# Two TensorE details of a four-layer kernel: logit sums by row halves, and an evenly shared tail in the output projection

## Chip, cores and metric

The kernel runs on one core of one Trainium2 chip. The metric is the device time of one execution in microseconds (us), lower is better; a program is timed several times and the median is compared. Times of single instructions and waits come from one profiled execution.

## What is computed

Four residual layers on a sequence of S = 2048 rows of width D = 576: attention, gated unit, attention, gated unit, with the same weights in both rounds.

```python
x = x + A(layernorm(x)); x = x + B(layernorm(x)); x = x + A(layernorm(x)); x = x + B(layernorm(x))

def A(x):                       # 32 heads of 18, window of 8 positions, every second one
    q, k, v = split(x @ wqkv)
    logits[h, s, w] = sum_d q[h, s, d] * k[h, s - 2 * w, d] * 18 ** -0.5      # masked before the start
    attn = softmax(logits, over w)
    return (sum_w attn[h, s, w] * v[h, s - 2 * w, :]) @ wo

def B(x):                       # F = 4608
    return ((x @ w_gate) * (x @ w_up)) @ w_down
```

## The kernel before

**Chunks.** The sequence is cut into chunks: the first four (j = 0 to 3) have 128 rows, the other fourteen (j = 4 to 17) have 256. A chunk j is one attention layer (`attention`) and the gated unit behind it (`glu`). Chunks of the first and of the second round alternate in groups of 1024 rows.

**Layout.** D = 576 is four full blocks of 128 and a tail of 64. The weights of the projections are permuted so that partition 32 * jj + h of a block holds head h; a block holds four of the 18 elements of each head, and the tail holds two, in its lower 64 partitions. The upper 64 partitions of the tail block (index KF = 4) are zero in q, k, v and, until the change, in `wo_p`.

**TensorE by row halves.** In chunks of 256 rows most products are issued as pairs: the helper `both` (L438) zips two lists, one of products that use partitions 0 to 63 (row half 0) and one for partitions 64 to 127 (row half 1). The two halves write different PSUM banks. Each bank gets contributions from both halves, so the work is done in two passes with the banks swapped, and between the passes a `fence` (L443) stands: ScalarE copies one element of the bank (L445, tile `tok`), and the first product of the second pass waits for that copy.

**PSUM slots.** Four slots `unit`, each of a bank in `pg` and its partner in `pu` (the fourth is `acct` and `pa`), are shared by all that runs on TensorE from j = 5 on: gated units (two slots a pair of units), projections (two), output projection (two), and the logit sums (one).

**The logits.** VectorE multiplies q by shifted k (L641) and adds blocks (L645 to L650), which leaves four tiles `s1` of 128 partitions. TensorE then sums over the partitions that belong to one head with a 0/1 matrix `Esel` (L656): 16 products of 128 rows by 32 columns, four of them side by side in the four column groups. The sums stand in one PSUM bank. `soft1` (L672) takes the maximum over the window (L676) and subtracts it into `Lt` (L677); ScalarE's exponential (L679), `soft2` (L683, L684) and `soft3` (L687) follow. In chunks of j >= 5 the result goes through DRAM to be spread (L707 to L712), and 15 VectorE operations (L727, L741) apply it to v and leave `oT`.

**The output projection of a chunk of 256 rows** (L752 to L774). `strip(i, r, hh, first)` lists the products of row half r for rows i and output half hh: five for r = 0 (four blocks and the tail), four for r = 1, since the tail stands in the lower partitions alone. Pass 1 gives row half 0 the first output half and row half 1 the second; pass 2 swaps them. VectorE adds the result to the residual (L751).

**Order of the work.** Nothing runs in the order of the program text: `op` records operations with an engine, a cost in ns, what they read and write, a priority and a slot to hold, and `Plan.run` (L79) writes each engine's queue by simulating those costs. The products of the gated units are a fixed chain (`bb`); attention is fitted in between, some chunks ahead. The plan adds TURN (L25) when TensorE goes between operations marked `half` and others. Each engine's queue then runs in that order on the chip, whatever the real durations.

Of the kernel before, what the change touches and what calls it, by code (L numbers as in the profile page):

```python
# [156 lines left out]
def kernel(  # L157
# [148 lines left out]
    def setup_b():  # L306
        def mk_zero():
            for t_ in qT_:
                nc.gpsimd.memset(t_[TL:P, KF, :], 0.0)
            for t_ in kv_:  # L310
                nc.gpsimd.memset(t_[TL:P, :, KF, :], 0.0)
            nc.gpsimd.memset(q_x[TL:P, KF, :], 0.0)
            nc.gpsimd.memset(kv_x[TL:P, :, KF, :], 0.0)
            for t_ in halo:
                nc.gpsimd.memset(t_[:], 0.0)
            nc.gpsimd.memset(wo_p[TL:P, KF, :], 0.0)
        op("POOL", 2600, mk_zero, w=[f"{x}{t}{i}" for x in "qkv" for t in (4, "H") for i in ZN] + [f"halo{i}" for i in range(n_al)] + ["wo_z"])
        for k in range(KT):
# [41 lines left out]
    def setup_wo():  # L360
# [3 lines left out]
        for dd in range(2):  # L364
            op("SP", 470, dma(wo_p[32 * dd:32 * dd + 32, KF, :], wv_[:, 16 + dd, :]), w=[f"wot{dd}"], nbytes=32 * D * 2, prio=2)

# [9 lines left out]

    wok = ["wo_z", "wot0", "wot1"] + [f"wo{dd}" for dd in range(4)]

# [88 lines left out]
    def attention(j, la, t0, nst):  # L467
# [164 lines left out]
        if not on_pe:  # L632
            pool["k"] = "unit"
        b1 = Bank()
        for p_ in range(W // 2):
            def l1(p_=p_):
# [15 lines left out]
            def esel(p_=p_, srcs=None):  # L652
                pav = wv(b1())
                for i_, s_ in enumerate(srcs()):
                    for jj in range(4):
# [12 lines left out]
        if not fast:  # L668
            op("PE", 250 + 4 * max(45, 0.215 * n), lambda: [esel(p_, lambda p_=p_: [late["s1"][p_]]) for p_ in range(W // 2)],
               r=["sel", "s10", "s11", "s12", "s13"], prio=0, margin=mg, **b1.take())  # L670
# [7 lines left out]
        op("DVE", 260 + 4.2 * n + (250 if t0 == 0 else 0), soft1, r=[b1.key] + (["cap"] if t0 == 0 else []), w=["Lt", "mx"], prio=prio - 1, **b1.drop())  # L678
        op("ACT", 109 + 1.66 * n, lambda: nc.scalar.activation(late["Lt"][:, 0:W * sq], late["Lt"][:, 0:W * sq], ACT.Exp),  # L679
# [72 lines left out]
        if nst == 2:  # L752
# [4 lines left out]
            def strip(i, r, hh, first):  # L757
                def one(t):
                    rows = slice(TL * r, TL * r + TL)
                    return nc.tensor.matmul(bank(hh, us[i])[:, 0:HD], lhsT=oT[rows, t, i * P:(i + 1) * P], rhs=wo_p[rows, t, hh * HD:(hh + 1) * HD],  # L760
                                     start=(first and t == 0), stop=(not first and t >= KF - 1), skip_group_check=True)
# [296 lines left out]
```

## Time and profile before

| what | value |
| --- | --- |
| time, median of 3 runs | 1064.89 us (1063.15 to 1067.89) |
| the profiled execution's own time | 1063.73 us |
| its span, first to last instruction | 1061.6 us, granted TensorE clock 0.996 |
| TensorE busy (PE) | 1036.8 us, 98% of the span |
| VectorE busy (DVE) | 782.6 us, 74% |
| ScalarE busy (ACT) | 407.5 us, 38% |
| GpSimd busy (POOL) | 16.4 us, all of it in the first 19 us |

How to read it: a busy TensorE is not TensorE at its peak, because the shown duration of a product reaches from its start to the end of its results and overlaps with the next ones. What counts on TensorE is the distance from one start to the next. Queues run in order, so a wait at the head of a queue holds all that stands behind it.

### The profile page before, as it was taken

The numbers are of one execution on the slowest core, as the hardware profiler recorded it, in microseconds if no ns is written. First come the engines' busy times: TensorE is split into PE (matmuls) and PEld (weight loads), VectorE is DVE, ScalarE is ACT, GpSimd is POOL, SyncE is SP. The second block draws the span as 40 slices with busy tenths as digits, with TensorE's granted clock in tenths as the row PEclk, the third lists the DMA queues.
The fourth block names the chain that finished last, engine by engine and source line by source line (L and its number), as shares of the span: only waits on it lengthen the run. The fifth ranks groups of instructions, "written<-read, shape, count | busy, mean of one in ns | idle before, by whom it ended". The sixth has DMA issues, their size and how long they took to land.

```text
span 1061.6 us, 39889 instructions
## 1 busy us (share of the span) xinstructions
PE 1036.8 (98%) x17832; PEld 834.5 (79%) x17832; DVE 782.6 (74%) x1420; ACT 407.5 (38%) x1080; POOL 16.4 (2%) x43
## 2 busy tenths in 40 slices
PE   5999999999999999999999999999999999999998
PEld 4787887788788889778888787877887788777775
DVE  6788998877989969797979753676788847733332
ACT  4742254244444453334433333334344252233231
POOL 6000000000000000000000000000000000000000
PEclk8999999999999999999999999999999999999999
DMA  9955554463335633335552534243252344343332
GB/s 267 333 170 166 183 148 134 130 143 111 82 107 103 163 76 123 107 94 121 141 130 69 154 99 105 90 128 94 84 158 82 98 90 125 115 127 102 117 99 68
DMA packets 146827, 133.67 MB, mean 126 GB/s; under 512 B 42272, under 2 KB 146016, under 8 KB 146656
## 3 DMA queue, kind: packets, MB, share of 16 engines
q1 hardware_dynamic: 146656, 131.13, 44.0%
q8 instruction: 139, 2.28, 0.9%
q14 instruction: 32, 0.26, 0.1%
HBM read 118.51 MB, written 4.06 MB: 115 GB/s over the span
## 4 chain that ended last, share of the span: by engine, by line
PE 75%; DVE 18%; DMA 4%; issue 1%; ACT 1%; SPq 1%; DVEq 0%; ACTq 0%
PE pu L855 14%; PE pg L855 14%; PE acct L855 5%; PE pu L923 5%; PE pa L923 5%; PE pa L855 5%; PE pg L923 4%; PE acct L923 4%; DVE scr L727 3%; DVE oT L741 3%; PE pg L501 3%; DVE h L867 3%; PE pu L501 3%; PE pu L831 3%; PE pg L831 2%; DVE scr L641 2%
## 5 line engine op out<-in xcount | busy, mean ns | idle before, releaser
L855 PEld LDWEIGHTS <-wg 64*128 64x128 bf16 x4032 | 366.4, 94 | 29.5 <-issue 2.9
L855 PE MATMUL pg<-xnT_B,wg 64*128 64x256 bf16 x3008 | 386.5, 269 | 0.9 <-DVE xf L751 0.9
L855 PE MATMUL pu<-xnT_B,wu 64*128 64x256 bf16 x3008 | 385.9, 269 | 0.3
L855 PEld LDWEIGHTS <-wu 64*128 64x128 bf16 x4032 | 365.7, 94 | 22.6 <-issue 1.0
L923 PEld LDWEIGHTS <-h 64*128 64x128 bf16 (+1 forms) x1992 | 118.1, 94 | 99.4 <-DVE h L867 2.7
L867 DVE TENSOR_TENSOR h<-pu,g_sb 128x512 bf16<-128x512 f32 x224 | 150.9, 685 | 55.3 <-ACT g_sb L866 51.9
L924 PE MATMUL pu<-wd,h 64*128 64x64 bf16 (+1 forms) x972 | 183.7, 189 | 1.0 <-DVE h L867 0.9
L924 PE MATMUL pg<-wd,h 64*128 64x64 bf16 (+1 forms) x972 | 183.8, 189 | 0.0
L866 ACT CAST g_sb<-pg 128x512 bf16<-128x512 f32 x224 | 130.0, 586 | 131.7 <-PE pg L855 87.6
L445 ACT COPY tok<-pu 1x1 f32<-1x1 f32 x276 | 40.6, 147 | 300.2 <-PE pu L855 202.8
L855 PE MATMUL acct<-xnT_B,wg 64*128 64x256 bf16 x1024 | 139.8, 269 | 0.0
L855 PE MATMUL pa<-xnT_B,wu 64*128 64x256 bf16 x1024 | 139.3, 269 | 0.1
L923 PE MATMUL pg<-wd,h 64*128 64x512 bf16 x528 | 136.4, 377 | 0.3 <-DVE h L867 0.3
L923 PE MATMUL pu<-wd,h 64*128 64x512 bf16 x528 | 136.5, 377 | 0.0
L923 PE MATMUL acct<-wd,h 64*128 64x512 bf16 (+1 forms) x468 | 121.3, 377 | 1.4 <-DVE h L867 1.4
L923 PE MATMUL pa<-wd,h 64*128 64x512 bf16 (+1 forms) x468 | 121.5, 377 | 0.0
L501 PEld LDWEIGHTS <-wqkv 64*128 64x128 bf16 (+1 forms) x2044 | 106.6, 96 | 15.7 <-issue 4.8
L924 PEld LDWEIGHTS <-h 64*128 64x128 bf16 (+1 forms) x1992 | 116.5, 95 | 0.8 <-issue 0.2
L641 DVE TENSOR_TENSOR scr<-qT,kv 128x2560 bf16<-128x2560 bf16 (+1 forms) x68 | 91.1, 1343 | 25.9 <-ACT kv L576 25.9
L501 PE MATMUL pg<-xnT_A,wqkv 64*128 64x256 bf16 (+2 forms) x916 | 103.6, 265 | 2.0 <-ACT xnT_A L430 2.0
L501 PE MATMUL pu<-xnT_A,wqkv 64*128 64x256 bf16 (+1 forms) x876 | 101.8, 267 | 0.3 <-DVE kv L574 0.3
L855 PE MATMUL pg<-xnT_B,wgu_t 64*128 64x256 bf16 x376 | 101.1, 269 | 0.0
(149 smaller groups left out, 1580.1 us busy)
## 6 DMA issues: line engine op xcount, KB each, us to landing
wd<-in_B_w_down_dram SPq DMA_DIRECT2D x324, 288.0 KB, 4.6
scr<-a_dram SPq DMA_DIRECT2D x52, 128.0 KB, 2.7
wg<-in_B_w_gate_dram SPq DMA_DIRECT2D x6, 768.0 KB, 10.2
wu<-in_B_w_up_dram SPq DMA_DIRECT2D x6, 768.0 KB, 11.0
out_dram<-xf SPq DMA_DIRECT2D x16, 144.0 KB, 3.8
xb<-in_A_x_dram SPq DMA_DIRECT2D x6, 288.0 KB, 2.8
a_dram<-scr SPq DMA_DIRECT2D x13, 128.0 KB, 2.4
scr<-in_A_wqkv_dram SPq DMA_DIRECT2D x4, 288.0 KB, 4.8
```

The lines of the kernel that those rows point to most:

```text
L445: box["at"] = nc.scalar.copy(tok[0:1, :], src())
L501: return nc.tensor.matmul(bank(p_, u)[0:m, e * n:(e + 1) * n], lhsT=wqkv[r_, k, w0:w0 + m], rhs=xnT_A[r_, k, c0:c0 + n], start=start, stop ...
L641: nc.vector.tensor_tensor(late["prod"][p_ % 2][:, :, :, 0:n], q2, k2, op=ALU.mult)
L727: nc.vector.tensor_tensor(js(dst), js(vT[:, :, o0:o0 + n]), abw, op=ALU.mult)
L741: op("DVE", 70 + 2.63 * n, lambda i_=i_: nc.vector.tensor_tensor(oT[:, :, 0:n], oT[:, :, 0:n], late["prod"][i_ % 2][:, 0, :, 0:n], op=ALU. ...
L831: nc.tensor.matmul(pt[:, e * n:(e + 1) * n], lhsT=w_[:, k, ft * P:(ft + 1) * P], rhs=xT[:, k, 0:n], start=(first and k == 0 and e == 0), s ...
L855: return nc.tensor.matmul(ps[:, e * n:(e + 1) * n], lhsT=w_, rhs=xT[rows, k, 0:n], start=(first and e == 0 and k == 0), stop=(not first an ...
L866: op("ACT", 490, lambda: nc.scalar.copy(g_sb[gs][:, 0:ul], pg[use["slot"]][:, 0:ul]), r=[f"wg_{j}_{u}"], w=[f"g{gs}"], prio=0, due=True)
L867: op("DVE", 605, lambda: nc.vector.tensor_tensor(hb[hs][:, 0:ul], pu[use["slot"]][:, 0:ul], g_sb[gs][:, 0:ul], op=ALU.mult), r=[f"wu_{j}_{ ...
L923: return [lambda: nc.tensor.matmul((pg, pu)[i][use["slot"]][:], lhsT=lhs, rhs=wt[rows, e % 2, 0:512], start=first, stop=fin, skip_group_ch ...
L924: lambda: nc.tensor.matmul((pg, pu)[i][tl["slot"]][:, 0:TL], lhsT=lhs, rhs=wt[rows, e % 2, 512:D], start=first, stop=fin, skip_group_check ...
```

## The change

1. **Logit sums of chunks j >= 5** (`split`): each of the 16 products is cut into two of 64 rows by 32 columns, one for each row half, so there are 32. Row half 0 writes the bank in `pg`, row half 1 its partner in `pu` of the same slot. ScalarE copies the `pg` bank into `Lt`; `soft1` adds the `pu` bank to it on VectorE, and its maximum and its subtraction now read `Lt` in SBUF. The plan marks the TensorE operation as `half`.
2. **Output projection of the 14 chunks of 256 rows**: the tail rows of `wo` are loaded a second time into the upper 64 partitions (two DMAs more), in place of a memset to zero. ScalarE copies the tail of `oT` for the second 128 rows into the upper partitions. The tail of the first 128 rows is then done by row half 0, that of the second 128 by row half 1: the strips have 5 and 4 products for i = 0, and 4 and 5 for i = 1. The strip with five goes first in each zip, and the fence reads the bank that it wrote.

```diff
-            nc.gpsimd.memset(wo_p[TL:P, KF, :], 0.0)
...
         for dd in range(2):
-            op("SP", 470, dma(wo_p[32 * dd:32 * dd + 32, KF, :], wv_[:, 16 + dd, :]), w=[f"wot{dd}"], nbytes=32 * D * 2, prio=2)
+            for r_ in (0, TL):
+                op("SP", 470, dma(wo_p[r_ + 32 * dd:r_ + 32 * dd + 32, KF, :], wv_[:, 16 + dd, :]), w=[f"wot{dd}{r_}"], nbytes=32 * D * 2, prio=2)
...
+        split = not on_pe
...
+                if split:
+                    s_ = srcs()[0]
+                    for jj in range(4):
+                        for r_, t_ in ((slice(0, TL), pav), (slice(TL, P), wv(pu[b1.use["slot"]]))):
+                            nc.tensor.matmul(t_[32 * jj:32 * jj + 32, 2 * p_:2 * p_ + 2, :], lhsT=Esel[r_, :], rhs=s_[r_, :, sq * jj:sq * (jj + 1)],
+                                             start=(p_ == 0), stop=True, skip_group_check=True)
+                    return
...
+        if split:
+            op("ACT", 490, lambda: nc.scalar.copy(wv(late["Lt"]), wv(b1())), r=[b1.key], w=["Lt"], prio=prio - 1)
...
             pav = wv(b1())
+            if split:
+                lt = wv(late["Lt"])
+                nc.vector.tensor_tensor(lt, lt, wv(pu[b1.use["slot"]]), op=ALU.add)
+                pav = lt
...
-                return [lambda t=t: one(t) for t in range(KF + 1 - r)]
+                return [lambda t=t: one(t) for t in range(KF + (i == r))]
+            op("ACT", 280, lambda: nc.scalar.copy(oT[TL:P, KF, P:2 * P], oT[0:TL, KF, P:2 * P]), r=["oT"], w=["oTt"], prio=prio)
...
-                    o = op("PE", KT * TILE * HD, lambda i=i, first=first: both(strip(i, 0, 0 if first else 1, first), strip(i, 1, 1 if first else 0, first),
-                                                                                           None if first else fs[i]),
+                    o = op("PE", (KF + 0.5) * TILE * HD, lambda i=i, first=first: both(*[strip(i, r, r if first else 1 - r, first) for r in (i, 1 - i)],
+                                                                                      None if first else fs[i]),
...
-                        fence(fs[i], lambda i=i: bank(0, us[i])[0:1, 0:1], [f"wo{j}_{i}"])
+                        fence(fs[i], lambda i=i: bank(i, us[i])[0:1, 0:1], [f"wo{j}_{i}"])
```

More of the change, by code (lines that the diff above doesn't have):

```diff
@@ L315, in mk_zero @@
                 nc.gpsimd.memset(t_[:], 0.0)
-            nc.gpsimd.memset(wo_p[TL:P, KF, :], 0.0)
-        op("POOL", 2600, mk_zero, w=[f"{x}{t}{i}" for x in "qkv" for t in (4, "H") for i in ZN] + [f"halo{i}" for i in range(n_al)] + ["wo_z"])
+        op("POOL", 2600, mk_zero, w=[f"{x}{t}{i}" for x in "qkv" for t in (4, "H") for i in ZN] + [f"halo{i}" for i in range(n_al)])
         for k in range(KT):
@@ L375, in setup_glu @@
             op("SP", 550, dma(wgu_t[TL:2 * TL, fs], B_w_up[KF * P:D, fs]), w=[f"wut{s}"], nbytes=TL * fw * 2, prio=4 + s)
-    wok = ["wo_z", "wot0", "wot1"] + [f"wo{dd}" for dd in range(4)]
+    wok = [f"wot{dd}{r_}" for dd in range(2) for r_ in (0, TL)] + [f"wo{dd}" for dd in range(4)]
     def head(src, keys, nst, dst, key, prio, ab, on_pe, mg, c0=0, halves=False):
@@ L669, in attention @@
             op("PE", 250 + 4 * max(45, 0.215 * n), lambda: [esel(p_, lambda p_=p_: [late["s1"][p_]]) for p_ in range(W // 2)],
-               r=["sel", "s10", "s11", "s12", "s13"], prio=0, margin=mg, **b1.take())
+               r=["sel", "s10", "s11", "s12", "s13"], prio=0, margin=mg, half=split, **b1.take())
+        if split:
+            op("ACT", 490, lambda: nc.scalar.copy(wv(late["Lt"]), wv(b1())), r=[b1.key], w=["Lt"], prio=prio - 1)
         def soft1():
             pav = wv(b1())
+            if split:
+                lt = wv(late["Lt"])
+                nc.vector.tensor_tensor(lt, lt, wv(pu[b1.use["slot"]]), op=ALU.add)
+                pav = lt
             if t0 == 0:
@@ L677, in soft1 @@
             nc.vector.tensor_tensor(wv(late["Lt"]), pav, mx_t[:, 0:sq].unsqueeze(1).to_broadcast([P, W, sq]), op=ALU.subtract)
-        op("DVE", 260 + 4.2 * n + (250 if t0 == 0 else 0), soft1, r=[b1.key] + (["cap"] if t0 == 0 else []), w=["Lt", "mx"], prio=prio - 1, **b1.drop())
+        op("DVE", 260 + 4.2 * n + (250 if t0 == 0 else 0) + (600 if split else 0), soft1, r=[b1.key] + (["Lt"] if split else []) + (["cap"] if t0 == 0 else []), w=["Lt", "mx"], prio=prio - 1, **b1.drop())
         op("ACT", 109 + 1.66 * n, lambda: nc.scalar.activation(late["Lt"][:, 0:W * sq], late["Lt"][:, 0:W * sq], ACT.Exp),
```

## The prediction

> **What bounds the kernel now.** I read the page's busy rows, the table of windows, the waits of TensorE, and then the timeline around the two places that change.
>
> ```profile
> span 1061.6 us, 39889 instructions
> PE 1036.8 (98%) x17832; PEld 834.5 (79%) x17832; DVE 782.6 (74%) x1420; ACT 407.5 (38%) x1080; POOL 16.4 (2%) x43
> ...
> PE 75%; DVE 18%; DMA 4%; issue 1%; ACT 1%; SPq 1%; DVEq 0%; ACTq 0%
> ```
>
> TensorE is never long without work, and three quarters of the chain that ended last are its own. The windows say where VectorE comes close (columns: window, its length, busy us of PE, PEld, DVE, ACT, POOL):
>
> ```profile
> 120.00:640.00 520.00, 515.36 (x8938) 421.01 (x8937) 438.98 (x770) 213.56 (x575) 0.00 (x0) 1.00 0.44 118
> 640.00:1000.00 360.00, 358.55 (x6334) 284.59 (x6332) 227.61 (x397) 126.24 (x353) 0.00 (x0) 1.00 0.38 108
> ```
>
> VectorE is 84% busy (439 of 520) up to 640 us and 63% after it; attention is prepared ahead there. TensorE waits for VectorE seldom (waits of TensorE, total us, times, longest):
>
> ```profile
> PE acct L923 <- DVE h L867: 1.4, 2, 0.8
> PE pu L924 <- DVE h L867: 0.9, 2, 0.7
> ...
> PE pg L855 <- DVE xf L751: 0.9, 2, 0.6
> ```
>
> So time is won where TensorE's stream gets shorter, and lost where its queue stands for a PSUM slot or an `h`.
>
> **Part 1, the output projection.** The timeline of the one at 728.77 us, its last rows (start, length):
>
> ```profile
> 730.86 0.28 PE L760 MATMUL pa<-wo_p,oT 64*128 64x288 bf16 x1
> 730.96 0.27 PE L855 MATMUL pg<-xnT_B,wg 64*128 64x256 bf16 x1
> 730.98 0.28 PE L760 MATMUL pa<-wo_p,oT 64*128 64x288 bf16 x1
> 731.07 0.27 PE L855 MATMUL pg<-xnT_B,wg 64*128 64x256 bf16 x1
> 731.10 0.28 PE L760 MATMUL pa<-wo_p,oT 64*128 64x288 bf16 x1
> 731.18 0.27 PE L855 MATMUL pg<-xnT_B,wg 64*128 64x256 bf16 x1
> 731.23 0.27 PE L855 MATMUL pu<-xnT_B,wu 64*128 64x256 bf16 x1
> ```
>
> Products of one row half follow each other at 122.5 ns (0.12 here). Row half 1 (`pg`) is already in the gated unit while row half 0 (`pa`, then `pu` of L855) still works off its 20 products: it leaves at 731.23, 2.46 us after 728.77, which is 20 x 122.5 ns. The lead of row half 1 (0.27 us) buys nothing: ahead of the logit sums at 237.51 the timeline has only one half running, and those sums need both. So a projection costs the count of row half 0. The change makes it 18 and 18: 2 x 122.5 = 245 ns less. In all 14 projections row half 0 takes its 20 products without a gap longer than one product, so the term is firm. One deduction: in 8 of them row half 1 enters within 10 ns of the other, in 6 it enters 89 to 91 ns late, and before it could catch up. There only 245 - 90 = 155 ns are won. Sum: 8 x 0.24 + 6 x 0.155 = 2.85, say **-2.9 us** (3.4 if the lag does not count).
>
> What could take it back is the fence. From the start of the last product of pass 1 to that of the first one of pass 2 there were 6 products (735 ns), now 5 (612). At 728.77 the last row-half-0 product before the first fence starts at +0.49 us, the ScalarE copy runs from 729.64 (+0.865) to +1.014, and a product held by it starts at +1.072, that is 58 ns later. The new need is at 9 x 122.5 = +1.10. It fits, by 30 ns. In two of 14 the copy came late (466.8 and 795.8 us, ScalarE held by other work); there the gain goes, 2 x 0.245 = 0.5. I keep -2.9 as the value and -2.4 as its weak end. The copy of `oT`'s tail on ScalarE, 64x128, lies between the row of `tok` (147 ns) and the 128x140 copies at L486 (309 ns): 14 x 0.3 = 4 us on an engine that is 38% busy, ahead of a projection that in the new queue stands at least 292 products of TensorE, some 16 us, ahead of its own gated unit. If that cover were gone, 0.3 us a chunk.
>
> **Part 2, the logit sums on TensorE.** A block of 16 products now looks like this (the second view is a chunk of 128 rows, with full 128-row products ahead):
>
> ```profile
> 237.31 0.27 PE L855 MATMUL pg<-xnT_B,wgu_t 64*128 64x256 bf16 x1
> 237.51 0.41 PE L656 MATMUL pg<-scr,Esel 128*32 128x128 bf16 x16
> 237.85 0.28 PE L855 MATMUL pu<-xnT_B,wu 64*128 64x256 bf16 x1
> ```
>
> ```profile
> 97.42 0.50 PE L831 MATMUL pg<-xnT_B,wg 128*128 128x128 bf16 x6
> 97.85 0.30 PE L656 MATMUL pa<-scr,Esel 128*32 128x64 bf16 x16
> ```
>
> From 237.31 to 237.85 are 539 ns, of which 109 are the product ahead, so a block costs 430 ns: 90 to get in (199 between starts less 109), four sets of four at 59 ns, 98 to get out (151 less the 53 of the last set). The plan credits the change with both turns (its TURN, 148 and 98), for it marks the block `half`. Does the row split make the turn? In the second view both sides have 128 rows and only the columns differ, 128 against 32: the last L831 starts at 97.70, its 128 columns take 56 ns, and the first sum comes at 97.85, so the gap is 0.09 as well. A change of columns alone costs the turn, and 64x128 to 64x32 is such a change. I take **0 us**: both turns stay, and the four sets stay four, each of eight products. Bounds: -13 x 188 ns = -2.4 if the turns go; +13 x 4 x 59 ns = +3.1 if the row halves do not run side by side with 32 columns, which no row shows.
>
> The Trainium skill (TensorEngine Tiling (Array Packing), Key Properties) says that changing the tiling mode, not just the tile, drains the engine, and lists 64x128 and 64x32 as two configurations; by it this part wins nothing on TensorE; were the row split alone the mode, it would win 2.4 us. The trace agrees, by the gap of 0.09 us above. The same list gives 64x32 eight tiles that work independently; no row here shows that.
>
> **Part 3, what the logit sums now need elsewhere.** ScalarE: 13 copies 128x512 out of PSUM at 586 ns (row L866) are 7.6 us. VectorE: 13 adds from PSUM and SBUF at 685 ns (row L867). The subtraction stays near 691 ns. The maximum now reads SBUF: no such row, but L683 reduces the same shape from SBUF in 1029 ns and L676 from PSUM in 684, so it costs 0 to 0.345 more; I take the upper one, for the same address pattern. Together 0.69 + 0.345 = 1.03 us, times 13 = 13.4 us on VectorE, some 8 us of it before 640, where it has 81 idle. The chain of attention gets about 1.8 us longer, which its place ahead hides.
>
> Two covers matter. The slot: before, it was free after maximum and subtraction, some 1.7 us after the last product began (0.22 its own length, 0.09 from a product's end to the start of the copy that waits for it, as at the fence above, 0.69 + 0.69). Now each bank goes when it is read: 0.22 + 0.09 + 0.59 + 0.1 + 0.69 = 1.7 us for the later one. In the new queue 6 of the 13 blocks have their slot used again after 52 products, 2.83 us at the spacing above, and the others later; before, one had 2.34 and three had 2.83, and no gap of TensorE stands behind those. The queue: behind the add stand the maximum, the subtraction, then mostly two `h` (L867) of the gated unit, and behind ScalarE's copy in most cases two `g_sb`. VectorE waits for the sums already (L676, 4.7 us in 6 times on `pg`); it now waits for ScalarE's 0.6 too. If an `h` becomes 1 us late in a phase with no free slot, TensorE stands; with the two smaller rows (L923 `pg` 0.3, L501 0.4) its waits for an `h` are 3.0 us in 6 times now. VectorE's load grows by under 2% and its queue at these 13 places by a second, so I add a fifth of that, **+0.6 us**. Bounds: -1.5 (the new order avoids half of those waits) and 13 x 1.03 = +13.4 (VectorE's whole extra falls on TensorE).
>
> **Start.** Two more DMAs on SP (0.47 us each, 37 KB each) stand ahead of the gated unit's first weights; these land from 21.4 to 26.3 us, and the first product that reads them starts at 44.6: nothing. GpSimd loses a memset of 0.57 us, at 4.18, on no path.
>
> **The sum.** -2.9 + 0 + 0.6 = -2.3 us. Against the profiled execution (span 1061.6, and 2.1 around it that nothing here touches): 1063.73 - 2.3 = 1061.4. The median of the runs is 1.16 above that execution, so I forecast **1062.6 us**, 0.2% less. A change under 0.5% (5.3 us) is about what a measurement of this kernel cannot tell from none.
>
> **Rivals.**
> - *The turns go* (the row split alone makes the mode): 1062.6 - 2.4 = 1060.2. Against it the gap of 0.09 us between two 128-row forms. 0.12.
> - *The row halves take turns with 32 columns*: eight sets for four, 1062.6 + 3.1 = 1065.7. For it: no row. Against it: with 128 columns the halves start 3 ns apart, and four column groups do too. 0.09.
> - *The longer softmax stands in the way of the gated unit's evacuation*, and the kernel is slower than before. Place: VectorE's queue behind the add, and ScalarE's behind the copy. It decides once an `h` comes later than the next pair of units needs its slot; at a mean of 0.5 us for each of 13 blocks, 6.5 us instead of 0.6: 1068.5. For it: VectorE 84% busy, its real durations above the plan's costs (the plan adds 600 ns for what I price at 1.03). Against it: slots are reused 2.8 us or more after the block. 0.15.
> - *The change doesn't do what it says*: the fence comes late in most projections, since only 30 ns are to spare, and the 245 ns turn into a wait: 1062.6 + 2.9 = 1065.5. 0.07.
>
> **Chances.** The forecast holds 0.57. Faster by over 0.5% (below 1059.6) needs the turns gone and fewer waits, or a lucky order: 0.14. Slower by over 0.5% (above 1070.2): half of the third rival with its tail, 0.14. Within: 0.72. The range is 1058.5 to 1068.5: the first two rivals and the fourth lie inside, the third about half.
>
> **What will show it.** Right: in each projection both row halves leave with 18 products, the next L855 of either 2.2 us after the first; the gaps at the logit sums stay near 0.09 and 0.10 us, with four sets at some 59 ns; L676's successor near 1.03 us; waits of TensorE on `h` below 5 us. Wrong: a block that costs much less or more than 430 ns, a wait on `tok` ahead of pass 2, or many waits on `h`.

## The result, and the profile after

The changed kernel took **1068.31 us** (median of 8 runs, 1064.35 to 1070.64), the kernel before 1063.98 beside it (8 runs): ratio **1.0035**, 95% interval 1.002 to 1.0051. It is slower by 0.35%, where 0.2% faster was forecast. The interval lies clear of 1, so eight runs beside eight do tell a change of this size from none, which the prediction doubted. The profiled execution took 1069.17 us (before: 1063.73).

The page of the changed kernel: span, busy rows, and the first line of the chain that ended last.

```profile
span 1067.1 us, 40312 instructions
PE 1038.7 (97%) x18040; PEld 872.2 (82%) x18040; DVE 795.0 (75%) x1433; ACT 418.4 (39%) x1107; POOL 15.8 (1%) x42
...
PE 68%; DVE 26%; DMA 3%; issue 1%; ACT 1%; SPq 1%; DVEq 0%; ACTq 0%
```

VectorE's share of the chain went from 18 to 26% while its busy time rose by only 12.4 us, near the 13.4 that were expected. So it is not that VectorE has too much to do; TensorE now waits for it more often. The windows put that in the first part, up to 640 us, where TensorE is busy for 511.4 us instead of 515.4:

```profile
120.00:640.00 520.00, 511.36 (x8989) 428.51 (x8984) 436.82 (x757) 217.66 (x582) 0.00 (x0) 1.00 0.44 118
640.00:1000.00 360.00, 358.10 (x6411) 300.36 (x6407) 239.95 (x421) 131.68 (x369) 0.00 (x0) 1.00 0.39 108
```

(Lines have moved: L855 is now L871, L867 L883, L751 L766, L903 L919, L760 L775, L641 L642; the split sums are L659.) What TensorE waits for, from 100 us on (total, times, longest):

```profile
PE pg L871 <- DVE xf L766: 2.0, 1, 2.0
PE pu L871 <- DVE h L883: 1.5, 3, 1.0
PE pu L871 <- DVE xf L919: 1.3, 3, 0.7
PE acct L871 <- DVE xf L766: 1.1, 1, 1.1
PE pg L847 <- DVE xf L766: 1.0, 1, 1.0
```

The whole view adds up to 10.3 us, against 5.8 before. Waits for an `h` went from 3.0 to 4.1. Waits for the residual adds behind the projection and the down product (`xf`, L766 and L919), which give a PSUM slot back, went from 1.8 to 5.4; the 1.8 before are the line of L855 in the prediction and this one:

```profile
PE pg L831 <- DVE xf L751: 0.9, 1, 0.9
```

This sum of the whole view, from 100 us to the end, is the measure used for all kernels below.

The two parts themselves did what was said of them. Both row halves leave a projection together, after 18 products (timeline; last product of the projection and first one behind it, the pair that began at 734.94):

```profile
737.89 0.28 PE L775 MATMUL pu<-wo_p,oT 64*128 64x288 bf16 x1
737.90 0.28 PE L775 MATMUL pg<-wo_p,oT 64*128 64x288 bf16 x1
738.02 0.27 PE L871 MATMUL pu<-xnT_B,wu 64*128 64x256 bf16 x1
738.02 0.27 PE L871 MATMUL pg<-xnT_B,wg 64*128 64x256 bf16 x1
```

The logit sums run side by side in both row halves, with both turns:

```profile
237.58 0.27 PE L871 MATMUL pu<-xnT_B,wgu_t 64*128 64x256 bf16 x1
237.78 0.23 PE L659 MATMUL pg<-scr,Esel 64*32 64x128 bf16 x1
237.78 0.23 PE L659 MATMUL pu<-scr,Esel 64*32 64x128 bf16 x1
...
238.13 0.28 PE L871 MATMUL pa<-xnT_B,wu 64*128 64x256 bf16 x1
```

From 237.58 to 238.13 are 549 ns (by the unrounded starts), where 539 were before: 0.01 us for a block, 0.1 for all 13, which are alike (548 to 562 ns).

The longest wait shows how the loss comes about. TensorE starts the last product of a projection at 540.02, does one step of the down product, and stands for 2.05 us; VectorE meanwhile begins a q.k product of another chunk, 1.48 us long, that its queue has ahead of the residual adds:

```profile
540.35 0.19 PE L940 MATMUL pa<-wd,h 64*128 64x64 bf16 x1
542.59 0.37 PE L871 MATMUL pg<-xnT_B,wg 64*128 64x256 bf16 x1 [2.05 <-DVE xf L766]
```

```profile
540.69 1.48 DVE L642 TENSOR_TENSOR scr<-qT,kv 128x2560 bf16<-128x2560 bf16 x1
542.09 0.45 DVE L766 TENSOR_TENSOR xf<-pg,xb 128x288 f32<-128x288 f32 x1
```

And the wait is not all it costs. Behind it the granted clock is 0.50 for 3.2 us, so another 1.6 us are lost in this execution (a row of the windows: the three numbers at its end are the mean granted clock, the DMA share and GB/s):

```profile
542.60:545.80 3.20, 3.20 (x27) 2.37 (x28) 3.13 (x10) 0.39 (x2) 0.00 (x0) 0.50 0.31 86
```

Whether the other seven runs have this is not shown: their mean granted clock is 0.995 to 0.997, here it is 0.992.

The account of the profiled run: the first product of the gated unit comes 0.7 us later (45.31 against 44.61 us), waits +4.5, the halved clock +1.6, the projection -2.6; that is 4.2 of the 5.5 us by which the span is longer. The 0.7 us are no price of the change: in the profiled executions of e1 to e11, n1 and n2 below, that product comes anywhere from 43.1 to 46.6 us. The -2.6 is measured from the first start to the last start of each projection plus one product (122.5 ns): the 14 take 32.05 us instead of 34.69, not counting the down products that the new queue has between the passes of two of them. The rest no view names singly; pauses of a tenth of a microsecond and of one row half alone are a guess.

### The profile page after: what moved, and what is told of

Its sections match the earlier page's. It is cut to its first block, busy times and chain, and to the rows that moved or that the text cites. A ratio compares the mean times of both kernels' runs of the same rounds, so it can differ in the third digit from the quotient of the medians.

```text
span 1067.1 us, 40312 instructions
## 1 busy us (share of the span) xinstructions
PE 1038.7 (97%) x18040; PEld 872.2 (82%) x18040; DVE 795.0 (75%) x1433; ACT 418.4 (39%) x1107; POOL 15.8 (1%) x42
## 4 chain that ended last, share of the span: by engine, by line
PE 68%; DVE 26%; DMA 3%; issue 1%; ACT 1%; SPq 1%; DVEq 0%; ACTq 0%
PE pu L871 13%; PE pg L871 12%; PE pg L939 8%; PE pu L939 8%; PE acct L871 5%; DVE oT L756 5%; DVE scr L742 5%; PE pa L871 5%; DVE h L883 4%; DVE scr L642 4%; PE pg L501 2%; PE pu L847 2%; PE pg L847 2%; PE pu L501 2%; DMA scr<-a_dram 1%
## 5 line engine op out<-in xcount | busy, mean ns | idle before, releaser
L871 PEld LDWEIGHTS <-wg 64*128 64x128 bf16 x4032 | 370.2, 94 | 24.8 <-issue 7.5
L871 PEld LDWEIGHTS <-wu 64*128 64x128 bf16 x4032 | 373.6, 94 | 17.5 <-issue 3.7
L871 PE MATMUL pg<-xnT_B,wg 64*128 64x256 bf16 x2928 | 383.3, 270 | 2.0 <-DVE xf L766 2.0
L871 PE MATMUL pu<-xnT_B,wu 64*128 64x256 bf16 x2928 | 381.7, 270 | 3.1 <-DVE h L883 1.5
L939 PE MATMUL pg<-wd,h 64*128 64x512 bf16 (+1 forms) x828 | 214.0, 378 | 0.8 <-DVE h L883 0.6
L939 PE MATMUL pu<-wd,h 64*128 64x512 bf16 (+1 forms) x828 | 214.2, 378 | 0.0
L883 DVE TENSOR_TENSOR h<-pu,g_sb 128x512 bf16<-128x512 f32 x219 | 147.5, 684 | 70.1 <-ACT g_sb L882 66.1
L939 PEld LDWEIGHTS <-h 64*128 64x128 bf16 (+1 forms) x1992 | 131.6, 94 | 83.0 <-DVE h L883 3.5
L940 PE MATMUL pu<-wd,h 64*128 64x64 bf16 (+1 forms) x828 | 157.0, 190 | 0.5 <-DVE h L883 0.5
L940 PE MATMUL pg<-wd,h 64*128 64x64 bf16 (+1 forms) x828 | 157.0, 190 | 0.0
L871 PE MATMUL acct<-xnT_B,wg 64*128 64x256 bf16 x1104 | 150.8, 270 | 1.1 <-DVE xf L766 1.1
L871 PE MATMUL pa<-xnT_B,wu 64*128 64x256 bf16 x1104 | 150.2, 269 | 1.0 <-DVE h L883 0.9
L940 PEld LDWEIGHTS <-h 64*128 64x128 bf16 (+1 forms) x1992 | 132.6, 95 | 0.8
L642 DVE TENSOR_TENSOR scr<-qT,kv 128x2560 bf16<-128x2560 bf16 (+1 forms) x68 | 91.1, 1343 | 15.1 <-ACT kv L576 15.1
L871 PE MATMUL pu<-xnT_B,wgu_t 64*128 64x256 bf16 x366 | 98.9, 270 | 0.0
L871 PE MATMUL pg<-xnT_B,wgu_t 64*128 64x256 bf16 x366 | 98.9, 270 | 0.0
L501 PE MATMUL pu<-xnT_A,wqkv 64*128 64x256 bf16 (+2 forms) x813 | 94.0, 266 | 0.8 <-DVE kv L574 0.5
L756 DVE TENSOR_TENSOR oT<-oT,scr 128x1280 bf16<-128x1280 bf16 (+1 forms) x119 | 90.9, 764 | 3.1
```

What stands on the lines that cost most here:

```text
L501: return nc.tensor.matmul(bank(p_, u)[0:m, e * n:(e + 1) * n], lhsT=wqkv[r_, k, w0:w0 + m], rhs=xnT_A[r_, k, c0:c0 + n], start=start, stop ...
L642: nc.vector.tensor_tensor(late["prod"][p_ % 2][:, :, :, 0:n], q2, k2, op=ALU.mult)
L756: op("DVE", 70 + 2.63 * n, lambda i_=i_: nc.vector.tensor_tensor(oT[:, :, 0:n], oT[:, :, 0:n], late["prod"][i_ % 2][:, 0, :, 0:n], op=ALU. ...
L871: return nc.tensor.matmul(ps[:, e * n:(e + 1) * n], lhsT=w_, rhs=xT[rows, k, 0:n], start=(first and e == 0 and k == 0), stop=(not first an ...
L883: op("DVE", 605, lambda: nc.vector.tensor_tensor(hb[hs][:, 0:ul], pu[use["slot"]][:, 0:ul], g_sb[gs][:, 0:ul], op=ALU.mult), r=[f"wu_{j}_{ ...
L939: return [lambda: nc.tensor.matmul((pg, pu)[i][use["slot"]][:], lhsT=lhs, rhs=wt[rows, e % 2, 0:512], start=first, stop=fin, skip_group_ch ...
```

## The experiments

Two kinds of cause stood against each other at the start: the projection change wins what it should and something else eats it, that is **waits of TensorE** by the new queue order or by VectorE's added work; or the time is that of one part alone, such as **the longer softmax**, a rival of the prediction that gives just this time (1068.5). The texts on record say what each theory expects of each run. Times are medians beside runs of the kernel before on the same chip; its medians in the five sets of runs were 1062.9, 1062.4, 1062.1, 1061.7 and 1064.9 us (1064.0 beside the changed kernel), so ratios are compared across sets. None of these kernels leaves out any of the computation.

| kernel | projection, sums | planned costs | us | ratio, 95% | TensorE's waits, us |
| --- | --- | --- | --- | --- | --- |
| before | old, old | old | 1062.9 | 1 | 5.8 |
| after | new, new | the change's | 1068.3 | 1.0035 (1.002-1.0051) | 10.3 |
| e1 | new, old | the change's | 1065.5 | 1.0035 (1.0022-1.0048) | 11.2 |
| e2 | old, new | the change's | 1070.3 | 1.008 (1.0054-1.0105) | 9.4 |
| e3 | new, old | order of after | 1063.4 | 1.0008 (0.9999-1.0018) | 8.7 |
| e4 | new, new | sums' true costs | 1062.5 | 0.9993 (0.9979-1.0008) | 6.2 |
| e5 | new, new | order of e1 | 1079.6 | 1.0159 (1.0146-1.0172) | 21.2 |
| e6 | new, old | order of before | 1067.1 | 1.0044 (1.0026-1.0061) | 10.9 |
| e7 | old, old | order of e1 | 1068.8 | 1.006 (1.004-1.008) | 9.9 |
| n1 | old, old | one number, 10 ns | 1064.0 | 1.0014 (1.0001-1.0028) | 5.4 |
| n2 | old, old | one number, 5 ns | 1061.6 | 0.9999 (0.9986-1.0013) | 4.8 |
| e8 | new, old, tail copy on VectorE | order of before | 1063.7 | 1.0024 (1.0009-1.0039) | 8.9 |
| e9 | new, new, tail copy on VectorE | order of after | 1070.9 | 1.0083 (1.0063-1.0103) | 13.1 |
| e10 | new, old, tail copy on VectorE | order of e1 | 1070.6 | 1.0081 (1.006-1.0102) | 12.9 |
| e11 | old, new | sums' true costs | 1066.6 | 1.0038 (1.0021-1.0055) | 8.3 |
| t1 | old, old | VectorE's true spacings | 1052.3 | 0.9914 (0.9899-0.9929) | 1.0 |
| t3 | new, old | VectorE's true spacings | 1048.8 | 0.9879 (0.9859-0.9899) | 1.4 |
| t2 | new, new | both | 1053.1 | 0.9923 (0.9908-0.9937) | 2.8 |
| t4 | old, new | both | 1053.3 | 0.9894 (0.9872-0.9915) | 2.3 |
| t5 | new, old | order of t2 | 1052.5 | 0.9884 (0.9865-0.9902) | 3.3 |

### Each part alone, and each order with the other work

**e1: the projection change alone.**

```diff
-        split = not on_pe
+        split = False
```

> The projection's shared tail alone, with the logit sums as before. Before is 1064.0 us, the changed kernel 1068.3. Theory W (work: the added ScalarE copies, VectorE adds and longer maxima make the gated unit's products and slots late): 1061 us, the 2.9 us that the projection saves and nothing else. Theory O (order: the plan puts the queues in a worse order because of the new costs, and the work itself is harmless): about 1061 too, as this plan has none of the new costs of the sums. Theory P (the projection's change itself, by its fences or by the order it brings, costs more than it saves): 1065 or more.

1065.5: slower by as much as the whole change, with VectorE's work untouched. So the longer softmax cannot be the whole cause. In its trace the 14 projections take 31.8 us where before has 34.7, measured as above, so the 2.9 us of the prediction are won; TensorE's waits are 11.2 us instead of 5.8. (The texts for e6, e7 and e8 name 3.3 us instead. That is the difference in all of TensorE's streaming time from 100 us on, and it is rough: the trace of e1 lacks the records of 14 down products that the trace of before has, and its gated unit starts 1.5 us earlier, at 43.14 us.)

**e3: the order of after, with the sums of before.** Every queue as in the changed kernel; the block is 16 products of 128 rows, and there is no copy and no add.

```diff
-                if split:
-                    ... (the split products)
-            op("ACT", 490, lambda: nc.scalar.copy(wv(late["Lt"]), wv(b1())), ...
+            op("ACT", 490, lambda: None, ...
-                nc.vector.tensor_tensor(lt, lt, wv(pu[b1.use["slot"]]), op=ALU.add)
```

> The changed kernel's queues in the changed kernel's order, but on the chip the logit sums are those of before: 16 products of 128 rows, no ScalarE copy, no VectorE add, maximum from PSUM. The plan still counts the new costs. Theory W: 1061 to 1062 us. Theory O: 1067 to 1068 us, as the changed kernel. In between if both take part.

1063.4, ratio 1.0008: with the sums' work taken out of the changed kernel, 0.27% (2.9 us) is gone. So that work costs 2.9 us there, a fifth of its 13.4 us on VectorE. But the longest wait of the changed kernel stands here too, at the same place and as long, with the clock at 1.00 behind it:

```profile
538.63 0.27 PE L860 MATMUL pg<-xnT_B,wg 64*128 64x256 bf16 x1 [2.05 <-DVE xf L755]
```

So the sums' work does not make this wait; it comes with the order.

**e5: the same work in the order of e1, where the plan knows nothing of it.** ScalarE's copy and VectorE's add are issued inside the softmax's own step, at no planned cost.

```diff
-            op("ACT", 490, lambda: nc.scalar.copy(wv(late["Lt"]), wv(b1())), ...
+                nc.scalar.copy(lt, pav)
                 nc.vector.tensor_tensor(lt, lt, wv(pu[b1.use["slot"]]), op=ALU.add)
-        ... + (600 if split else 0), soft1
+        ... + 0, soft1
```

> The queues of the kernel with the projection's change alone, in exactly that order, with the new work of the logit sums put in at its places (32 products of 64 rows, the ScalarE copy, the VectorE add, the maximum from SBUF), which the plan does not count. Theory W: 1067 to 1069 us, or more, for the plan knows nothing of the work. Theory O: 1061 to 1062 us.

1079.6, 14.1 us over e1 and 21.2 us of waits: where the plan does not know of it, VectorE's 13.4 us costs the kernel about its whole length. That was the upper end of the prediction's bounds for the waits.

**e4: after, with the true costs in the plan.** The work is that of the changed kernel.

```diff
-            op("ACT", 490, lambda: nc.scalar.copy(wv(late["Lt"]), wv(b1())), ...
+            op("ACT", 590, lambda: nc.scalar.copy(wv(late["Lt"]), wv(b1())), ...
-        ... + (600 if split else 0), soft1
+        ... + (1115 if split else 0), soft1
-  margin=mg, half=split, **b1.take())
+  margin=mg, **b1.take())
```

> The changed kernel, with the plan told what the trace shows: 590 ns for the ScalarE copy (490 before), 1115 ns more for the softmax's first step (600 before), and the turns of TensorE counted at the logit sums. Theory W as pure load: about 1068 us still. Theory W with the plan's too low prices as its point (queues late against the plan): 1063 to 1065. Theory O: another order, anything from 1061 to 1069.

1062.5, 0.42% under the changed kernel, with nothing changed but what the plan believes (just under the range of the theory that these prices are the point). From here the question was what the plan does not know.

**e6: the new projection in the order of before.** The passes of 18 products, ScalarE's copy issued with the last add of the attention, the plan as it was.

```diff
-                return [lambda t=t: one(t) for t in range(KF + 1 - r)]
+                return [lambda t=t: one(t) for t in range(KF + (i == r))]
+                    if i_ == W - 1 and nst == 2:
+                        nc.scalar.copy(oT[TL:P, KF, P:2 * P], oT[0:TL, KF, P:2 * P])
```

> The kernel before with the projection's new work alone (18 and 18 products, the tail rows in both halves, ScalarE's copy of the tail), put in without the planner knowing: the order of every engine's queue is the one of before, but for the copy. Before on this chip ran at 1062.9. Theory 'order': the work is worth the 3.3 us by which TensorE's streaming time after the first 100 us is shorter in e1's trace, and what e1 lost was stalls of its new order (+5.6 us): 1059.6, between 1058.5 and 1061. Theory 'copy': ScalarE's 14 copies of 296 ns hold up the copies that the gated unit waits for: near e1's time, 1064.5 to 1066. Theory 'no gain': a half that ended early was already filled by the next products, so nothing is won: 1062.5 to 1063.3.

1067.1: above every theory's figure. The waits of ScalarE and those of TensorE say why:

```profile
ACT oT L743 <- DVE oT L741: 23.4, 14, 3.4
```

```profile
PE pu L857 <- ACT tok L444: 3.2, 3, 1.3
PE pa L925 <- ACT tok L444: 1.8, 1, 1.8
```

ScalarE stands 23.4 us at the tail's copy, for an attention that VectorE finishes later than the plan has it, and the fence's tokens queue behind: 5.7 us of TensorE in all, before it none.

**e7: the order of e1, with the old projection in it.**

```diff
-                return [lambda t=t: one(t) for t in range(KF + (i == r))]
+                return [lambda t=t: one(t) for t in range(KF + 1 - r)]
-            op("ACT", 280, lambda: nc.scalar.copy(oT[TL:P, KF, P:2 * P], oT[0:TL, KF, P:2 * P]), ...
+            op("ACT", 280, lambda: None, ...
```

> The exact queue order of e1 (projection change alone) with the projection's work of before in it (20 and 16 products, no copy of the tail): the new order without the new work. Theory 'order': e1's 1065.5 plus the 3.3 us of work that is back: 1067.5 to 1069.5. Theory 'copy': the copy was what held it up, and it is gone: 1062.5 to 1064. Theory 'no gain': the work is worth nothing either way, so e1's time: 1065 to 1066.

1068.8, by the ratios 0.25% (2.7 us) over e1, as the theory of the order had it, though the two are of different sets and their intervals overlap. At one order the new projection wins about what it should; the order itself cost 0.6%.

**e2: the split sums alone.** The changed kernel with the projection of before (its fence, load and memset too).

```diff
-                return [lambda t=t: one(t) for t in range(KF + (i == r))]
-            op("ACT", 280, lambda: nc.scalar.copy(oT[TL:P, KF, P:2 * P], oT[0:TL, KF, P:2 * P]), ...
+                return [lambda t=t: one(t) for t in range(KF + 1 - r)]
-                    o = op("PE", (KF + 0.5) * TILE * HD, ...
+                    o = op("PE", KT * TILE * HD, ...
```

> The split logit sums alone (part 2 with ScalarE's copy and VectorE's longer softmax, the plan counting them as the change does), with the projection of before. Theory 'order and late VectorE': the sums' added VectorE work costs what it added to e1 in the changed kernel, 2.9 us, and the new order draws its own stalls: 1064.5 to 1069. Rival (my prediction's price, nearly all of it hidden): 1062.5 to 1064.

1070.3, above the range of either theory: e1 and e2 do not add up to the changed kernel, they are each as slow as it or slower.

**n1 and n2: the old work, one number of the plan changed.**

```diff
-            op("DVE", 70 + 2.63 * n, pv, ...
+            op("DVE", 80 + 2.63 * n, pv, ...
```

```diff
-                    op("DVE", 370, lambda i=i, hh=hh: res(bank(hh, us[i]), i, hh), ...
+                    op("DVE", 365, lambda i=i, hh=hh: res(bank(hh, us[i]), i, hh), ...
```

> The kernel before with the same work and one number of the plan changed: VectorE's attention products are planned 10 ns longer each (743 to 753 ns, where the trace has 820). Only the order of the queues differs. Theory 'order': an order is a draw that is worth some us either way, so this differs from the 1062.9 of before by 1 to 5 us, with no work changed. Rival: orders near the one of before cost the same, and e1's loss was special to the projection's new costs: within 1 us of 1062.9.

> The kernel before with the same work; one number of the plan is changed by 5 ns: the residual adds behind the projection are planned at 365 instead of 370 ns (back to back they follow each other by 365 in the trace). TensorE's queue then differs from that of before in as many places as with the projection change. Theory 'an order is a draw': the time moves by 1 to 6 us with no work changed, most likely up (1063 to 1068), since the draws so far with unchanged work gave 1064.0 and 1068.8 against 1062.4. Rival 'only a worse model draws a worse order': a number that is nearer to the trace leaves the time within 1 us of 1062.4 or below.

1064.0 and 1061.6. The first is undecided between the two theories (its interval starts at 1.0001). The second redraws TensorE's queue in nearly as many places as e1 does (by the traces, 1070 of its 3048 attention products stand elsewhere among those of the gated unit, in e1 1216), and nothing happens. So "every new order is a draw worth some us" is too simple, and that theory falls; e7's order is bad, n2's is not.

### Where the tail's copy stands

**e8, e9, e10: the copy on VectorE**, behind the add that makes its data, in the exact orders of before, after and e1.

```diff
-                        nc.scalar.copy(oT[TL:P, KF, P:2 * P], oT[0:TL, KF, P:2 * P])
+                        nc.vector.tensor_copy(oT[TL:P, KF, P:2 * P], oT[0:TL, KF, P:2 * P])
```

> The projection's new work in the queue order of before, as in the run before (1067.1), but the copy of the tail is on VectorE, right behind the add that makes it, so no engine waits for another at it: 14 copies of a 64x128 bfloat16 tile on VectorE instead of ScalarE. In that run ScalarE's copies waited 23.4 us in 14 times for VectorE's attention, and TensorE then waited 5.7 us for ScalarE's fence tokens queued behind them. Theory 'copy' (the wait of ScalarE's queue took the gain): the work's gain shows, 1062.4 - 3.3 = 1059.1, plus up to 0.7 for VectorE's copies: 1058.5 to 1061. Rival 'work' (18 and 18 products in this order are themselves slower, by the fence or by the halves that no longer fill each other's ends): 1066 to 1068. In between, 1062 to 1063: the work is worth nothing and the copy cost 4.7.

> The changed kernel with its exact queue order, and the one edit that the copy of the projection's tail leaves ScalarE's queue (where it waited 10.0 us in 10 times for VectorE's attention) for VectorE, behind the add that makes it. Theory 'copy': the changed kernel's loss is in good part the wait of ScalarE's queue at it: 1063 to 1066 instead of 1068.3. Rival 'late VectorE': the stalls come from residual adds and products h that are late in VectorE's own queue, and 14 copies more there change nothing or add 0.5 to 2: 1068 to 1070.

> The projection change alone in its own order (1065.5 before), with the copy of the tail on VectorE instead of ScalarE. There ScalarE waited 10.3 us in 9 times for VectorE at the copy, but TensorE's waits for tokens were only 0.6. Theory 'copy': 1062 to 1064. Rival 'order': the loss of 5.6 us is stalls of the order (h, residual adds), which this leaves: 1065 to 1066.5.

In the order of before the waits for tokens vanish and 0.2% with them (e8 against e6, with overlapping intervals), but the residual adds come later instead (waits for `xf` 4.6 us after 2.1), and the gain still does not show in the time, which falls in none of the three ranges. In TensorE's queue it does: the 14 projections of e8 take 31.9 us instead of 34.7. This is also the kernel that puts the fence to the test, for 13 of them have their two passes back to back, and in none does pass 2 start late; in e6, where ScalarE has the tail's copy too, it is 0.25 us late in two of 14. In the other two orders, where ScalarE's wait had been planned for, moving the copy makes it worse than either rival had it, by 0.48% (e9) and 0.46% (e10): 14 copies of 189 ns, 2.6 us of VectorE that the plan does not know of, cost more than their own length. Why e10 loses as much as 5 us was not settled.

### A plan that knows VectorE

**e11: e2 with the edit of e4.**

```diff
-            op("ACT", 490, lambda: nc.scalar.copy(wv(late["Lt"]), wv(b1())), ...
+            op("ACT", 590, lambda: nc.scalar.copy(wv(late["Lt"]), wv(b1())), ...
-        ... + (600 if split else 0), soft1
+        ... + (1115 if split else 0), soft1
```

> The split sums alone (1070.3 before, with the plan counting 600 ns for the longer softmax, 490 for ScalarE's copy and no turn around the products), with the plan told what the traces show: 1115 ns, 590 ns and the turns. The same work, other queue order. Theory 'undercounted VectorE' (the loss is stalls for VectorE work which the plan does not know of, up to 0.5 us at each of 13 places, and what queues behind): 1063 to 1066. Rival 'work' (13.4 us of VectorE work costs TensorE some 8 us wherever it is put): 1069 to 1071.

1066.6, 0.42% under e2: the same step as from after to e4, though a little short of the theory's range.

That left VectorE's other costs. The trace has its attention back to back (changed kernel, one round of q.k work):

```profile
533.40 1.48 DVE L642 TENSOR_TENSOR scr<-qT,kv 128x2560 bf16<-128x2560 bf16 x1
534.92 0.69 DVE L646 TENSOR_TENSOR scr<-scr 128x1024 bf16<-128x1024 bf16 x1
535.64 0.42 DVE L650 TENSOR_TENSOR scr<-scr 128x512 bf16<-128x512 bf16 x1
```

Start to start these are 1.52 and 0.72 us. The plan has 1401 and 599 ns. An instruction that needs the one before it starts some 34 ns behind its end; one that doesn't starts 80 to 89 ns ahead of it (an `h` is some 684 ns long and an attention product behind it starts 600 after it, and the plan's 605 fits). The plan has the second kind's costs for the first kind's work: 118 ns short in each of four q.k products, 126 in each of their first sums, 108 in each of eight products with v (851 against 743), 138 in the softmax's second part (1656 against 1518). That is 4 x 118 + 4 x 126 + 8 x 108 + 138 = 1.98 us in each of 14 chunks.

**t1, t3, t2, t4: these four spacings told to the plan**, for the work of before, of the projection change, of both, of the sums (the last two with the sums' costs of e4 as well, 1066 for 1115).

```diff
-            op("DVE", 70 + 5.2 * n, l1, ...
+            op("DVE", 188 + 5.2 * n, l1, ...
-                op("DVE", 82 + 2.02 * n, l2, ...
+                op("DVE", 208 + 2.02 * n, l2, ...
-            op("DVE", 70 + 2.63 * n, pv, ...
+            op("DVE", 178 + 2.63 * n, pv, ...
-        op("DVE", 520 + 3.9 * n, soft2, ...
+        op("DVE", 658 + 3.9 * n, soft2, ...
```

> The work of before, planned with what VectorE takes in the attention when an instruction needs the one before it, as the trace of before spaces them start to start: q.k products 1519 ns instead of 1401, their first sums 725 instead of 599, products with v 851 instead of 743, the softmax's second part 1656 instead of 1518; 1.9 us for a chunk. Theory 'truth': a plan that knows VectorE better draws an order with fewer stalls: 1057 to 1061. Rival 'draw': any order is worth some us either way whatever the plan knows: 1062 to 1069.

> The projection change alone (1065.5) with the four spacings of VectorE's attention in the plan. Theory 'truth': 1056 to 1060, that is the run with the work of before and the same costs less 3 us. Rival 'draw': 1062 to 1069, with no fixed distance to that run.

> The changed kernel with the true costs of its sums in the plan (1062.5 in that run) and in addition the same four spacings of VectorE's attention. Theory 'truth': TensorE's shorter projection shows at last, 1056 to 1060, faster than both kernels. Rival 'draw': 1062 to 1069.

> The split sums alone, with the projection of before, planned with their true costs and with the four spacings of VectorE's attention. It completes a table of four kernels in which the plan knows VectorE: work of before 1052.3, projection change 1048.8, both changes 1053.1. Theory 'two separate prices' (the projection's work is worth 3.4, the sums' VectorE work costs 4.2, whatever the other part does): 1056.5, between 1055 and 1058. Rival 'draw': the sums' 4.2 is the order's, and this lands anywhere from 1050 to 1062, near 1052 if the sums cost nothing by themselves.

t1 gives 1052.3 us with no work changed, 0.86% under before, and t3 1048.8, which is faster than both kernels by over 1%. With t2 all three lie 3 to 7 us below the range of the theory 'truth', which had the direction and not the size. **The projection change is worth 0.35% there (3.5 us between two kernels of one set, each in the order of its own plan), near the prediction's -2.9.** The waits of TensorE in t3 after 100 us, the whole view, and its first window:

```profile
PE pg L871 <- ACT xnT_B L430: 0.9, 1, 0.9
PE acct L900 <- issue: 0.5, 3, 0.2
```

```profile
120.00:640.00 520.00, 518.37 (x9103) 427.73 (x9109) 432.16 (x751) 214.83 (x584) 0.00 (x0) 1.00 0.43 120
```

No wait for VectorE is left, though VectorE is busy for 788.9 us, 4.7 more than in e1. TensorE is busy for 518.4 of 520 us, where the changed kernel had 511.4. Not all of the gain is such waits: in t1 and t3 the first product of the gated unit comes at 41.73 and 41.34 us, 2.9 and 3.3 us ahead of before, where the sum from 100 us on does not see it. t4 fell on the side of the theory that the sums cost nothing by themselves (1053.3, by its ratio 0.2% under t1).

**t5: the order of t2 with the sums of before**, the edit of e3 made on t2.

> The exact queue order of the 1053.1 us kernel (both changes, true costs) with the logit sums of before in it: 16 products of 128 rows, no ScalarE copy, no VectorE add. So the new sums' 13.5 us of VectorE work and 7.6 of ScalarE work are taken out and the order stays. Theory 'the work has a price': near the projection change alone, 1048 to 1050. Rival 'the order has it' (the plan left room for that work, which then stands idle): 1052 to 1053.5.

1052.5, ratio 0.9884. By microseconds it equals t2, by the ratio it is 0.39% faster, for the two sets ran on different chips. So the price of the split sums in a plan that knows VectorE stays open: t4 against t1 says -0.2%, t2 against t3 +0.44%, t5 against t2 -0.39% for taking them out.

### All kernels together

Fitting the 20 rows (ratio times 1062.9) by TensorE's waits, the new projection and the new sums gives 1053.2 + 1.67 us for each us of waits, -4.3 for the projection, -0.2 for the sums, with 2.2 us of scatter; without e5, the far point, 1.89, -4.4 and +0.3. Without t1 to t5, which gain at the start too, it is 1.24, -3.3 and +0.8, with 1.0 us of scatter. The waits come from one execution each, so this is rough, but it puts the projection near the prediction's price, and the time goes with the waits. A slope over one is in keeping with the halved clock behind long waits, and with pauses too short for the view; neither was tested.

## Why the prediction was wrong, step by step

- **The projection, -2.9 us, "firm": right as work.** From first product to last the 14 projections take 2.6 us less in the changed kernel, 2.9 in e1 and 2.8 in e8; in time, e7 lies 2.7 us above e1 and t1 3.5 us above t3. It was not firm as time: in the orders of before (e6, e8) and of e1, longer waits took it and more. The two deductions, the fence with 30 ns to spare and the lagging half, cost little: waits for tokens are 0.5 us in the changed kernel. But the new plan put products between pass 1 and pass 2 there, in most projections eight of the gated unit in each half (0.87 us), so the fence wasn't tested. In e8 it was, and the 30 ns sufficed in all 13 projections that run through; in e6 they failed in two of 14, as many as the prediction set aside. So the rival by which the fence comes late in most projections is out. Six of the 13 in e8 take 2.29 to 2.30 us and five 2.21 to 2.22, the 0.09 us that the prediction gave the lagging half (the other two pause 0.23 us within pass 1).
- **The logit sums on TensorE, 0: right.** Both turns stay, the row halves run side by side (549 against 539 ns). The rivals "turns go" and "halves take turns" are out.
- **The added VectorE work, 13.4 us: the size was right.** The maximum from SBUF takes 1039 ns, the add 640 to 689, and VectorE's busy time rose by 12.4. VectorE also stands longer ahead of this step, 12.6 us in 7 times for ScalarE's copy where it stood 4.7 in 6 times on `pg` and 1.2 once on `acct`; e4 has the same 12.6 us, so this alone does not make the kernel slow.
- **The waits, +0.6 us: this is the step that failed.** "I add a fifth of that" was a fraction of VectorE's extra at 13 places. Measured: +4.5 us of waits and 1.6 us of halved clock behind one of them, in the profiled run. Two errors are in it. The term was tied to the sums alone, but the projection change by itself takes the waits from 5.8 to 11.2 us (e1), because its new costs re-plan every queue, and that order has 9.9 us of waits even with the old work in it (e7); the prediction worked out the new queue only around the 13 blocks and 14 projections. And it watched `h`: "waits of TensorE on `h` below 5 us" came true (4.1), while the loss came by the residual adds, from 1.8 to 5.4 us.
- **The tail's copy on ScalarE, "if that cover were gone, 0.3 us a chunk": too small.** In the changed kernel ScalarE waits 10.0 us in 10 times at that copy, which does little harm there, for the plan knew of it. In e6, where it did not, TensorE lost 5.7 us. A waiting instruction's price is not its length but what stands behind it.
- **The rival that gave the right time, 1068.5 by the longer softmax, is only partly the cause.** Its work costs 2.9 us in that order (e3 against after); in e4, where the plan has its true costs, the whole change comes out at the time of before (0.9993). Its argument, "real durations above the plan's costs", was the right clue for the wrong reason: the greater gap, 1.98 us a chunk, lay in the attention that was there before, and t1 to t5, planned without it, are all 0.8 to 1.2% under before. That the time lies inside the range of 1058.5 to 1068.5, at its end, is luck: the range reached so far only by this rival.

What stays open: why the order of e1 is bad and that of n2 isn't, though both differ from before in nearly as many places; and the sums' own price, above.

## What to carry to other kernels

Where a plan fixes each engine's queue, price the waits of the new order first: a saving on the busiest engine shows only if the engine that feeds it keeps to the plan. Compare planned costs with start-to-start spacings in the trace, apart for instructions that need the one before them and those that don't; here putting four such numbers right was worth 9.4 us, about three times what the projection change can win. Then test a change of work with the order held fixed, and a change of order with the work held fixed: neither alone told the truth here.

## What the hardware showed that was not expected

- **A wait of TensorE of 1.4 to 2 us can halve its clock for 3 us.** After waits of 2.05, 1.69, 2.05, 2.05 and 1.39 us (after, e2, e5, e10, and e11 at 538.6 us) the mean granted clock of the next 3.2 us was 0.50, 0.55, 0.65, 0.72 and 0.58; after waits of 2.05, 1.80, 2.05 and 2.20 us (e3 at 538.6, e1 at 813.9, e9 at 542.4, e5 at 193.4) it stayed 1.00. At 0.50, the gated unit's products of 64 rows follow each other at 214 ns instead of 109. The Trainium skill (TensorE: Matmul & The Clock Gate, HAM oscillation — how this bites in real kernels) puts the bound at idle gaps above about 3.4 us; here shorter ones did it, and the measurement decides. The same page of the Trainium skill (What's actually happening) describes a free-running window; that would fit that equal waits did and didn't do it, which no run here tests.
- **VectorE's durations are not what it costs its queue**: 34 ns more than the duration where the next instruction needs the result, 80 to 89 ns less where it doesn't (after, attention and `h`).
- **The maximum over the same 128x512 block takes 684 ns from PSUM (before) and 1039 from SBUF (after).** The prediction took this from the row of a sum; that it holds for the maximum is new.
